# Attention and two MoE layers on one core: the score matmuls of the third and fourth batch written for two tiles of queries at a time

## The chip, the core and the metric

The kernel runs on one core of one Trainium2 chip. Its time is the device time of one execution in microseconds (us), the median of several runs. A core has a matrix engine (TensorE, PE in the profile, with its weight loads shown apart as PEld), a vector engine (VectorE, DVE), a scalar engine (ScalarE, ACT), a general engine (GpSimd, POOL) and a queue engine (SyncE, SP) that here issues nearly all DMAs. Each engine executes its own instructions in the order in which they stand in its program, and waits where an operand or a buffer isn't ready; what stands behind a waiting instruction on the same engine waits with it. Matmuls write to banks of PSUM, and a bank can be written anew only when its last reader is through.

## The reference

Attention over 4 batches of 12 heads (448 queries, head size 64), with queries and keys normalised, and behind it two MoE layers over all 1792 tokens. Cut to what is computed:

```python
q_n, k_n = rmsnorm(q, g_q), rmsnorm(k, g_k)
scores = q_n @ k_n.T / sqrt(64)
attn = exp(scores - max(scores));  attn = attn / (attn.sum() + 1e-9)
x = (attn @ v)                       # -> 1792 x 768
g = x @ w_gate;  val = x @ w_val     # 768 -> 1536
x = (silu(g) * val) @ w_out          # 1536 -> 768
h = x @ w_in                         # 768 -> 2048
out = (h * cos(h)) @ w_out2          # 2048 -> 768
```

## The kernel before, in words

All values are float32 outside; inside, a float32 operand is split into two float16 parts, and a product is three float16 matmuls. Two heads are taken at a time (a pair): one in partitions and columns 0 to 63, the other in 64 to 127. A batch has 6 pairs, and a pair has 7 tiles of queries (64 queries of both heads), so that a batch has 42 tiles.

The scores of one tile are four matmuls with 64 columns of weights each and 448 columns moving, into one PSUM bank: two (one per head) with weights from `T`, the transposed and split queries and keys, and two with weights from `W`, a copy of `T` with its halves swapped. `s_mm` writes them. Behind them, for the tile, `s_max` takes the largest score of a row on DVE, `s_exp` (line 518) reads the bank once more on ACT and writes `pr`, and that frees the bank; then `pr` is split into float16 parts (`p`, line 542 and a subtraction on DVE or POOL), transposed by a DMA (`PT`), and multiplied with the values (`t<-PT,vh` and `t<-PT,vl`, again with 64 columns of weights). The banks of the scores are a pool of three, `ps_s`, which the small matmuls for the scales of the weights (`nm`) share; a tile's matmuls wait until the bank of three allocations before is free.

The first and second batch's scores stand at the start of the program and are written by another function. Those of the third and of the fourth batch are computed while the matrix engine works at the first MoE layer of the batches before them: the loop over `visits` writes, at each visit of a piece of weights (gate, value, output), some calls of `step`, which for a running number `n` calls `s_mm(n)`, `s_max`, `s_exp` and the later parts for tiles some steps back, and then the MoE matmuls (`mm<-xy,wp`, 128 columns of weights) into two banks of the pool `ps_m`, which has four. When a piece is through, `fin_gate` (lines 1153 and 1154) or `fin_val` (line 1162) reads these two banks on ACT and DVE, and its last reading on DVE (`ga`) frees them. DVE also converts the weights of later pieces to split form (`w<-raw`, `w<-raw,w`, then `wp<-w`).

The order of instructions on an engine isn't the order in which they are written: a scheduler sets it when the program is built, after its own estimate of when operands come ready. `tc.keep_in_program_order(r)` pins an instruction behind the one that was written just before it on the same engine. The helper `InOrder` does so for all instructions of an engine while the engine's name is in the set `in_order`; for PE this holds until the fourth visit, so that in the third and fourth batch the scheduler sets PE's order.

All operations that go through the helper have the line number 166 in the profile.

Of the kernel before, what the change touches and what calls it, by code (L numbers as in the profile page):

```python
# [174 lines left out]
def kernel(ctx: ExitStack, tc, q, k, v, g_q, g_k, w_gate, w_val, w_out, w2_in, w2_out, out):  # L175
    nc = tc.nc
    in_order = set()
    sync = InOrder(tc, nc.sync, "SP", in_order)
    gps = InOrder(tc, nc.gpsimd, "POOL", in_order)
    pe = InOrder(tc, nc.tensor, "PE", in_order)  # L180
    vec = InOrder(tc, nc.vector, "DVE", in_order)
    dve = InOrder(tc, nc.vector, "DVE0", in_order)
    B, H, S, D = q.shape
# [11 lines left out]
    HP = P // 2  # L195
# [22 lines left out]
    ps_s = ctx.enter_context(tc.tile_pool(name="ps_s", bufs=3, space=PSUM))  # L218
# [13 lines left out]
    def bank(pool, tag):  # L232
        return pool.tile([P, 512], F32, tag=tag, name=tag)
# [70 lines left out]
    NS = 2 * S // P  # L304
# [9 lines left out]
    slot = {}  # L314
# [172 lines left out]
            )  # L487

    def s_mm(n):
        g, t = divmod(n, NS)  # L490
        pg = prep[g]
        if t == 0:
            sms[g] = pools["sm"].tile([P, 3, 8], F32, tag="sm", name="sm")
        ps = bank(ps_s, "s")
        T, W = pg["T"], pg["W"]
        for i in range(2):
            for h in ((0, 1), (1, 0))[i]:
                hs = slice(HP * h, HP * h + HP)
                pe.matmul(
                    ps[hs, :S].rearrange("p (t q) -> p t q", q=HP), (T, W)[i][:, t, hs], T[:, NS:, hs],  # L500
                    start=(i == 0), stop=(i == 1),
                )
        slot[n] = ps

    def s_max(n):
        g, t = divmod(n, NS)
# [356 lines left out]
    def step(n, b):  # L863
        if b == 0:
            c_step(n)
        elif NB * b <= n < NB * (b + 1):
            s_mm(n)
            s_max(n)
            s_tail(n, b, 0)
            s_exp(n)  # L870
            s_tail(n, b, 1)
            s_prep(n)
        elif n >= 0:
            s_tail(n, b, 0)
            s_tail(n, b, 1)
        else:
            s_prep(n)
# [587 lines left out]
    for n in range(NBEGIN * NS - LEAD, NCB + CXX + CXL + 1):  # L1465
# [6 lines left out]
        i = n - EARLY  # L1472
# [44 lines left out]
    for bn, per in blocks:  # L1517
# [15 lines left out]
        for qn in range(per):  # L1533
            i = i0 + qn
# [53 lines left out]
    for c in range(NH):  # L1588
        j0 = j
        j += 2  # L1590
        for b in range(B):
            ps = [bank(ps_s, "s"), bank(ps_t, "t")] if nh % 3 == 2 else [bank(ps_m, "mm") for _ in range(2)]
# [41 lines left out]
    ps = {}  # L1634
# [55 lines left out]
```

## Time and profile before

| what | value |
|---|---|
| time, median of 3 runs | 1250.65 us (1249.37 to 1251.18) |
| profiled execution | 1257.0 us, of it 1255.2 us the span on the core |
| mean granted TensorE clock | 0.984 of full |
| busy | PE 1171.8 us (93%), DVE 944.2 us (75%), ACT 711.4 us (57%), POOL 377.2 us (30%) |
| scores of the third batch on PE | about 217 to 476 us of the span |
| scores of the fourth batch on PE | about 530 to 660 us of the span |

A row of the timeline reads: start in us, duration from the first start to the last end, engine, line, operation, output from inputs, partitions x columns of the weights, size and type of the output, and x with the number of instructions alike in a row; in brackets stands the idle time of the engine just before and who ended it. On PE the durations overlap, since one matmul flows in while another flows out; the rate is read from the starts.

### The profile page before, as it was taken

Reading aid. Unit: us, or ns where it says so; the run is one execution under the profiler, and the core shown is the slowest. Engines: PE = TensorE matmul, PEld = TensorE weight load, DVE = VectorE, ACT = ScalarE, POOL = GpSimd, SP = SyncE. Lnnn points to the kernel's source line nnn. Section 1 sums busy time; section 2 is a strip of 40 time slices with the busy share of each in tenths; the row PEclk is TensorE's granted clock in tenths of the full one; section 3 lists DMA queues with packets and bytes.
Section 4 is the critical chain, followed back from the end, with each engine's and each line's share of the span. In section 5 each row is a group of like instructions: output and inputs, shape, how many; then the busy total and the mean of one; then the engine's idle time right before and its main releaser. Section 6 shows DMA issues by size and latency. Waiting matters only on the chain. (4 is left out here: it accounts for less than half of the span.)

```text
span 1255.2 us, 18124 instructions
## 1 busy us (share of the span) xinstructions
PE 1171.8 (93%) x6294; PEld 658.5 (52%) x6294; DVE 944.2 (75%) x1778; ACT 711.4 (57%) x1356; POOL 377.2 (30%) x309
## 2 busy tenths in 40 slices
PE   2888988999998999999999999999999999999998
PEld 1333333445763447844468544865555554666655
DVE  7888865697668897068864498657888788999882
ACT  4878875545665653356653355457677667666220
POOL 7734503535322265035553012612112221100000
PEclk9989999999999999999999999999999999999999
DMA  7476665368767879589767687770522235222122
GB/s 189 113 187 191 174 190 162 81 187 251 191 197 216 216 194 308 180 180 232 158 139 238 231 307 284 263 245 9 209 69 76 89 139 201 63 95 76 51 70 88
DMA packets 220304, 211.47 MB, mean 168 GB/s; under 512 B 147124, under 2 KB 177716, under 8 KB 220212
## 3 DMA queue, kind: packets, MB, share of 16 engines
q1 hardware_dynamic: 220208, 210.31, 58.0%
q8 instruction: 49, 0.80, 0.3%
q14 instruction: 43, 0.35, 0.1%
q10 hardware_dynamic: 4, 0.00, 0.0%
HBM read 138.38 MB, written 41.57 MB: 143 GB/s over the span
## 5 line engine op out<-in xcount | busy, mean ns | idle before, releaser
L166 PE MATMUL mm<-xy,wp 128*128 128x448 f16 x2484 | 492.7, 355 | 8.2 <-DVE ga L1154 5.3
L166 PEld LDWEIGHTS <-wp 128*128 128x128 f16 x2880 | 278.0, 99 | 282.3 <-issue 38.6
L166 PE MATMUL mm<-g,wp 128*128 128x448 f32 x864 | 185.0, 371 | 1.9 <-DVE ga L1162 1.9
L166 PEld LDWEIGHTS mm<-g,wp 128*128 128x128 f32 x864 | 161.8, 190 | 21.2 <-issue 4.2
L166 DVE SCALAR_TENSOR_TENSOR w<-raw,w 128x768 int32<-128x768 int32 x136 | 144.9, 1071 | 1.2
L166 DVE TENSOR_REDUCE sm<-s 128x1 f32<-128x448 f32 x168 | 100.4, 614 | 50.6 <-PE s L166 50.4
L166 PEld LDWEIGHTS <-g 128*128 128x128 f16 x840 | 82.1, 98 | 55.4 <-DVE tmp L166 0.7
L166 POOL TENSOR_TENSOR g<-ga,g 128x448 fp32r<-128x448 f32 x48 | 67.0, 1406 | 144.4 <-ACT g L1164 144.1
L166 POOL TENSOR_TENSOR g<-tmp,g 128x224 f16<-128x224 f32 x64 | 48.0, 753 | 199.2 <-ACT g L1281 198.9
L518 ACT ACTIVATE pr<-s,sm,esc 128x448 f32<-128x448 f32 x84 | 60.4, 720 | 78.2 <-DVE sm L166 70.3
L166 PE MATMUL s<-T 128*64 128x448 f16 x336 | 63.6, 394 | 27.7 <-DVE T L166 16.9
L166 POOL TENSOR_TENSOR wp<-w,wp 128x768 fp32r<-128x768 f32 x36 | 70.7, 1971 | 58.5 <-ACT wp L1042 39.7
L166 DVE TENSOR_SCALAR w<-raw 128x768 int32<-128x768 int32 x68 | 49.4, 731 | 48.4 <-POOL wp L166 14.1
L166 PEld LDWEIGHTS <-T 128*64 128x64 f16 (+1 forms) x432 | 28.2, 109 | 104.6 <-issue 82.9
L166 POOL TENSOR_TENSOR ri<-ss,half 128x14 f32<-128x14 f32 x24 | 64.1, 2673 | 52.7 <-DVE ss L166 51.3
L973 ACT ACTIVATE raw<-w 128x768 f32<-128x768 f32 x56 | 47.0, 838 | 43.5 <-DVE w L166 30.7
L1274 ACT ACTIVATE tmp<-tmp 128x448 f32<-128x448 f32 x64 | 36.3, 571 | 50.3 <-DVE tmp L1273 49.2
L166 POOL TENSOR_TENSOR p<-pr,p 128x448 f16<-128x448 f32 x36 | 39.9, 1114 | 82.0 <-ACT p L542 63.3
L166 PE MATMUL mm<-wp,g 128*128 128x384 f16 x360 | 62.1, 326 | 0.6 <-DVE tmp L166 0.4
L166 POOL TENSOR_TENSOR h<-rqk,h 128x448 f16<-128x448 f32 x32 | 37.4, 1176 | 82.1 <-ACT h L447 52.8
L166 PE MATMUL s<-wp,g 128*128 128x384 f16 x360 | 61.9, 326 | 0.0
L166 PE MATMUL t<-pr,cV 128*128 128x448 f32 (+1 forms) x96 | 51.8, 623 | 9.1 <-ACT pr L722 8.5
(197 smaller groups left out, 1930.5 us busy)
## 6 DMA issues: line engine op xcount, KB each, us to landing
raw<-in_moe_w_out_dram SPq DMA_DIRECT2D x28, 768.0 KB, 5.7
raw<-in_moe_w_in_dram SPq DMA_DIRECT2D x16, 768.0 KB, 6.8
raw<-in_moe_w_gate_dram SPq DMA_DIRECT2D x12, 768.0 KB, 6.7
raw<-in_moe_w_val_dram SPq DMA_DIRECT2D x12, 768.0 KB, 5.3
wp<-scr_gate SPq DMA_DIRECT2D x24, 384.0 KB, 4.1
w<-scr_out SPq DMA_DIRECT2D x24, 384.0 KB, 3.8
wp<-scr_val SPq DMA_DIRECT2D x24, 384.0 KB, 5.3
y<-tmp SPq DMA_DIRECT2D x30, 224.0 KB, 3.8
```

What stands on the lines that cost most here:

```text
L166: r = f(*args, **kw)
L518: nc.scalar.activation(e, slot.pop(n)[:, :S], AF.Exp, bias=sm[:, 1, t:t + 1], scale=esc, accum_out=sm[:, 2, t:t + 1],)
L973: nc.scalar.activation(sq_dst[0], w32, AF.Square, accum_out=n[:, 0:1])
L1274: nc.scalar.activation(r, r, AF.Abs)
```

## The change

`s_mm(n)` at an even tile of a pair (0, 2, 4, 6) takes the banks of that tile and of the next, and writes the matmuls of both, eight in a row, each but the first pinned behind the one before it. At an odd tile it returns at once. Tile 6 has no partner and is written alone. So the pair's 28 matmuls are written as runs of 8, 8, 8 and 4 in place of seven runs of 4. The scheduler may still put other matmuls between two of a run. The instructions themselves are the same in kind and number on every engine.

```diff
     def s_mm(n):
+
         g, t = divmod(n, NS)
         pg = prep[g]
         if t == 0:
             sms[g] = pools["sm"].tile([P, 3, 8], F32, tag="sm", name="sm")
-        ps = bank(ps_s, "s")
+        if t % 2:
+            return
         T, W = pg["T"], pg["W"]
-        for i in range(2):
-            for h in ((0, 1), (1, 0))[i]:
-                hs = slice(HP * h, HP * h + HP)
-                pe.matmul(
-                    ps[hs, :S].rearrange("p (t q) -> p t q", q=HP), (T, W)[i][:, t, hs], T[:, NS:, hs],
-                    start=(i == 0), stop=(i == 1),
-                )
-        slot[n] = ps
+        run = []
+        for m in range(t, min(t + 2, NS)):
+            ps = slot[n + m - t] = bank(ps_s, "s")
+            for i in range(2):
+                for h in ((0, 1), (1, 0))[i]:
+                    hs = slice(HP * h, HP * h + HP)
+                    r = pe.matmul(
+                        ps[hs, :S].rearrange("p (t q) -> p t q", q=HP), (T, W)[i][:, m, hs], T[:, NS:, hs],
+                        start=(i == 0), stop=(i == 1),
+                    )
+                    if run and "PE" not in in_order:
+                        tc.keep_in_program_order(r)
+                    run.append(r)
```

On PE, the first two tiles of the third pair of the third batch (at 293.79 and 297.80 us in the trace before). `s_3054` is the bank of tile 0, `T_2850` and `W_2949` the pair's weights, `mm_3014` a bank of the MoE matmuls. Before:

```order
L166 LDWEIGHTS T_2850
L166 MATMUL s_3054<-T_2850 64x448
L166 LDWEIGHTS W_2949
L166 MATMUL s_3054<-T_2850,W_2949 64x448
L166 LDWEIGHTS W_2949
L166 MATMUL s_3054<-T_2850,W_2949 64x448
L166 LDWEIGHTS wp_2741
L166 MATMUL mm_3014<-xy_1312,wp_2741 128x448
```

The same place after, where `s_3059` is the bank of tile 1:

```order
L166 LDWEIGHTS W_2949
L166 MATMUL s_3054<-T_2850,W_2949 64x448
L166 LDWEIGHTS T_2850
L166 MATMUL s_3059<-T_2850 64x448
L166 LDWEIGHTS T_2850
L166 MATMUL s_3059<-T_2850 64x448
L166 LDWEIGHTS W_2949
L166 MATMUL s_3059<-T_2850,W_2949 64x448
L166 LDWEIGHTS W_2949
L166 MATMUL s_3059<-T_2850,W_2949 64x448
L166 LDWEIGHTS wp_2741
L166 MATMUL mm_3014<-xy_1312,wp_2741 128x448
```

Tile 1 stood 18 MoE matmuls later before, in a run of four of its own; now it follows tile 0 directly. Counted over the whole program, stretches of 64-column matmuls (scores, products with the values, or both) between two 128-column matmuls are 82 before (44 of them in the third batch, 38 in the fourth) and 64 after (29 and 35). Some runs of eight are cut by the scheduler: of the fourth batch's first tile one matmul stands some 160 matmuls ahead of the other three.

On DVE, the same pair (at 299.98 to 308 us in the trace before). `sm_3053<-s_3054` and `sm_3053<-s_3099` are the row maxima of tiles 0 and 1, `ga_2974` and `ga_2977` the readings of line 1162 that free two MoE banks, `W_3363<-T_3266` the copies for a later pair. Before:

```order
L166 TENSOR_REDUCE sm_3053<-s_3054 128x1
L166 TENSOR_SCALAR sm_3053<-sm_3053,nesc_96 128x1
L166 TENSOR_TENSOR p16_3106<-pr_3065,p16_3106 128x448
L1162 SCALAR_TENSOR_TENSOR ga_2974<-ga_2974,gs_2972,mm_3014 128x448
L1162 SCALAR_TENSOR_TENSOR ga_2977<-ga_2977,gs_2972,mm_3015 128x448
L166 TENSOR_REDUCE sm_3053<-s_3099 128x1
L166 TENSOR_SCALAR sm_3053<-sm_3053,nesc_96 128x1
L166 COPY W_3363<-T_3266 64x896 x2
L166 TENSOR_TENSOR h16_3545<-rqk_3263,h16_3545 128x7x64
```

The same place after (line 1169 is what line 1162 was):

```order
L166 COPY W_3363<-T_3266 64x896 x2
L166 TENSOR_TENSOR h16_3545<-rqk_3263,h16_3545 128x7x64
L166 TENSOR_REDUCE sm_3053<-s_3054 128x1
L166 TENSOR_REDUCE sm_3053<-s_3059 128x1
L166 TENSOR_SCALAR sm_3053<-sm_3053,nesc_96 128x1 x2
L1169 SCALAR_TENSOR_TENSOR ga_2974<-ga_2974,gs_2972,mm_3014 128x448
L1169 SCALAR_TENSOR_TENSOR ga_2977<-ga_2977,gs_2972,mm_3015 128x448
L166 TENSOR_TENSOR p16_3106<-pr_3070,p16_3106 128x448
```

The two copies and the subtraction for a later pair now stand ahead of the maxima of tiles 0 and 1 and of the two `ga`.

On DVE again, near the end of the third batch (457.91 to 468.30 us in the trace before). `ga_4712`, `ga_4715` and `ga_4789` are readings of line 1154 that free MoE banks, `w32_` the conversions of later weights. Before:

```order
L166 SCALAR_TENSOR_TENSOR wp_4686<-w32_4484,wsc_101,wp_4686 128x768
L166 TENSOR_SCALAR w32_4682<-raw_4583 128x768
L1154 SCALAR_TENSOR_TENSOR ga_4712<-ga_4712,mm_4602 128x448
L166 TENSOR_SCALAR w32_4795<-raw_4647 128x768
L166 SCALAR_TENSOR_TENSOR w32_4682<-raw_4583,w32_4682 128x768
L1154 SCALAR_TENSOR_TENSOR ga_4715<-ga_4715,mm_4603 128x448
L166 TENSOR_REDUCE sm_4365<-s_4718 128x1
L166 SCALAR_TENSOR_TENSOR w32_4795<-raw_4647,w32_4795 128x768
L166 TENSOR_SCALAR w32_4832<-raw_4753 128x768
L166 SCALAR_TENSOR_TENSOR w32_4682<-raw_4583,w32_4682 128x768
L166 TENSOR_SCALAR sm_4365<-sm_4365,nesc_96 128x1
L166 SCALAR_TENSOR_TENSOR w32_4795<-raw_4647,w32_4795 128x768
```

After, where `ga_4717` and `ga_4720` are the same two readings of the banks `mm_4602` and `mm_4603`:

```order
L1161 SCALAR_TENSOR_TENSOR ga_4717<-ga_4717,mm_4602 128x448
L166 TENSOR_SCALAR nm_4638<-s_4635 128x1
L166 TENSOR_SCALAR nm_4638<-nm_4638 128x1
L166 TENSOR_SCALAR winv_100<-nm_4638 128x1
L166 RECIPROCAL wsc_101<-winv_100 128x1
L1166 TENSOR_SCALAR gs_4715<-winv_100,vsc_102,gs_4715 128x1
L1161 SCALAR_TENSOR_TENSOR ga_4720<-ga_4720,mm_4603 128x448
L1166 TENSOR_SCALAR gs_4787<-winv_100,vsc_102,gs_4787 128x1
L166 TENSOR_TENSOR p16_4725<-pr_4729,p16_4725 128x448
L166 SCALAR_TENSOR_TENSOR wp_4643<-w32_4427,wsc_101,wp_4643 128x768
L166 SCALAR_TENSOR_TENSOR wp_4691<-w32_4484,wsc_101,wp_4691 128x768
L166 TENSOR_SCALAR w32_4687<-raw_4588 128x768
```

Both readings stand ahead of the weights' scaling and of the conversions now, where before they stood among these.

## Rows read from the trace of the kernel before

**Rows 1.** The page: busy us, share of the span and instructions of each engine.

```profile
PE 1171.8 (93%) x6294; PEld 658.5 (52%) x6294; DVE 944.2 (75%) x1778; ACT 711.4 (57%) x1356; POOL 377.2 (30%) x309
```

**Rows 2.** Busy time by stretch: window, length, busy of each engine, PEclk, DMA share, GB/s.

```profile
254.00:300.00 46.00, 44.25 (x244) 21.04 (x244) 43.63 (x76) 22.85 (x45) 21.81 (x13) 0.96 0.76 214
347.00:400.00 53.00, 48.05 (x251) 28.95 (x248) 36.90 (x82) 32.05 (x70) 11.45 (x9) 0.94 0.73 203
400.00:476.00 76.00, 71.08 (x409) 34.86 (x410) 70.56 (x125) 38.89 (x77) 33.27 (x22) 1.00 0.83 220
530.00:600.00 70.00, 69.12 (x410) 31.11 (x407) 51.28 (x108) 40.94 (x89) 28.16 (x22) 1.00 0.88 204
```

**Rows 3.** PE's timeline, a run of four scores and an idle stretch.

```profile
297.52 0.35 PE L166 MATMUL mm<-xy,wp 128*128 128x448 f16 x1
297.80 0.38 PE L166 MATMUL s<-T 128*64 128x448 f16 x2
298.01 0.36 PE L166 MATMUL s<-T,W 128*64 128x448 f16 x2
298.30 0.74 PE L166 MATMUL mm<-xy,wp 128*128 128x448 f16 x3
```

**Rows 4.** PE's timeline, a run of eight scores that stands in before already.

```profile
527.76 2.06 PE L166 MATMUL mm<-xy,wp 128*128 128x448 f16 x10
529.75 0.38 PE L166 MATMUL s<-T 128*64 128x448 f16 x2
...
530.34 0.35 PE L166 MATMUL s<-T,W 128*64 128x448 f16 x2
530.63 3.58 PE L166 MATMUL mm<-xy,wp 128*128 128x448 f16 x18
```

**Rows 5.** What PE waited for, 217 to 490 us: total us, times, longest us.

```profile
PE s L166 <- ACT pr L518: 6.5, 3, 3.2
PE mm L166 <- DVE ga L1154: 5.3, 4, 2.0
PE mm L166 <- DVE ga L1162: 1.9, 2, 1.5
```

**Rows 6.** PE's timeline, waits late in the third batch and just behind it.

```profile
464.71 6.59 PE L166 MATMUL mm<-xy,wp 128*128 128x448 f16 x34 [2.00 <-DVE ga L1154]
472.10 6.02 PE L166 MATMUL mm<-xy,wp 128*128 128x448 f16 x31 [0.80 <-DVE ga L1154]
...
487.00 0.68 PE L166 MATMUL mm<-g,wp 128*128 128x448 f32 x2 [1.54 <-DVE ga L1162]
```

**Rows 7.** DVE's timeline, where line 1162 frees banks near 281 us.

```profile
280.37 0.67 DVE L1162 SCALAR_TENSOR_TENSOR ga<-ga,gs,mm 128x448 f32<-128x448 f32 x1
...
282.95 2.68 DVE L166 SCALAR_TENSOR_TENSOR w<-raw,w 128x768 int32<-128x768 int32 x3
```

**Rows 8.** DVE's timeline at the third pair's first tiles.

```profile
299.98 0.62 DVE L166 TENSOR_REDUCE sm<-s 128x1 f32<-128x448 f32 x1
...
304.14 0.62 DVE L166 TENSOR_REDUCE sm<-s 128x1 f32<-128x448 f32 x1
...
306.77 0.79 DVE L166 COPY W<-T 64x896 f16<-64x896 f16 x2 [1.77 <-DMA T<-h]
307.60 0.62 DVE L166 TENSOR_TENSOR h<-rqk,h 128x448 f16<-128x448 f32 x1
```

**Rows 9.** PE's timeline, the wait at 347 us.

```profile
346.86 0.38 PE L166 MATMUL s<-T 128*64 128x448 f16 x2 [3.21 <-ACT pr L518]
```

**Rows 10.** DVE's timeline, 460 to 467 us.

```profile
460.24 0.61 DVE L1154 SCALAR_TENSOR_TENSOR ga<-ga,mm 128x448 f32<-128x448 f32 x1
460.77 1.65 DVE L166 TENSOR_SCALAR w<-raw 128x768 int32<-128x768 int32 x1
462.34 1.78 DVE L166 SCALAR_TENSOR_TENSOR w<-raw,w 128x768 int32<-128x768 int32 x1
464.05 0.61 DVE L1154 SCALAR_TENSOR_TENSOR ga<-ga,mm 128x448 f32<-128x448 f32 x1
```

## The prediction, as it was written before the change was run

> **What bounds the kernel now.** I read the page's busy shares first: PE is busy 1171.8 of 1255.2 us [rows 1], so what PE does not have to do, or does not have to wait for, is the only thing that can shorten the program by much. Then the table by stretch [rows 2], since the change touches two of them. In the fourth batch (530 to 600 us) PE is busy 69.12 of 70 us with DVE at 51.28: here PE alone is the bound, and a saving on PE should come through. In the third batch it isn't so. From 254 to 300 DVE is busy 43.63 of 46 us and from 400 to 476 it is 70.56 of 76, as close to full as PE, and from 347 to 400 PE idles 5 us. The view of waits says for whom [rows 5]: for banks that ACT's exponential frees (6.5 us in three waits) and for banks that DVE's `ga` frees (5.3 and 1.9). A saving on PE ahead of such a wait makes the wait longer and nothing else, so the third batch is counted apart from the fourth.
>
> **What one merger saves.** PE's timeline gives the price of leaving the 128-column matmuls for a run of scores and coming back. Matmuls in a stream start 0.19 us apart (ten in 2.06 us, the last 0.35 long, [rows 4]). Around a run of four, the last matmul before starts at 297.52 and the first one behind at 298.30 [rows 3]: 0.78, of which 0.19 would pass anyway, so 0.59. Around the run of eight the last matmul before starts at 527.76 + 9 x 0.19 = 529.47, the first behind at 530.63 [rows 4]: 1.16, so 0.97. Two fours made one eight save 2 x 0.59 - 0.97 = 0.21 us. The two ways into and out of the run are what is saved: they take 0.28 and 0.29 in place of 0.19.
>
> The Trainium skill ("TensorEngine Tiling (Array Packing)", Key Properties) says more strongly that changing the tiling mode drains TensorE, and "TensorE: Matmul & The Clock Gate", Single matmul latency, gives the constant part of a lone matmul as some 166 ns; an estimate by that is 2 x 0.166 = 0.33 us a merger and 6.0 us for the eighteen below. Rows 3 and 4 show 0.09 to 0.10 us a change, not 0.166, and the sum goes by them.
>
> **How many mergers.** Written in pairs, 84 runs of four would become 48 runs. The order gives less, since in before some runs stand together or beside products with the values already, and in after the scheduler cuts some: 82 stretches become 64. That is 15 fewer in the third batch and 3 in the fourth: 3.15 and 0.63 us, 3.8 together. Nothing is added or taken on any engine; all else is order.
>
> **What moves on the other engines.** (a) A tile's maximum and exponential come in twos, and the second tile of a run needs its bank one step earlier than before. With three banks the lines that PE waits for there are the exponentials, 6.5 us in before [rows 5]; the pair's first tile is computed no later than before, its second earlier, so I count no more than (b) and (c) for it.
>
> (b) Near 281 us the two `ga` of line 1162 stood at 280.37 and a little later, ahead of three conversions of weights that take 2.68 us [rows 7]; now conversions stand ahead. The banks they free are wanted by the next piece but one. Bounds 0 (PE comes late) and 2.7; DVE is 95% busy there, so it can't catch up, and I take 1.5, a little over the middle.
>
> (c) At the third pair's first tiles the copies `W<-T` and the subtraction `h` now stand ahead of two maxima and two `ga`. In before the copy waited 1.77 us for its DMA and ran at 306.77, the subtraction at 307.60 [rows 8], which ends near 308.2. Two maxima (0.62 each, [rows 8]) and their scaling behind it put the first `ga` near 309.6, where it was near 303.0, between the maxima at 299.98 and 304.14: 6.6 us late if the DMA lands as before. That DMA stands earlier on SP's queue too, behind a store and ahead of several transposes; if it comes up to 4 us sooner the delay is 2.7. Queued behind the waiting copy are all of DVE's later work, the exponentials of both tiles on ACT, and the third tile's run on PE, which wants the first tile's bank. Bounds 0 and 6.6; I take 2.7.
>
> (d) Between 460 and 472 us the opposite happens. PE waited 2.00 and 0.80 us for `ga` of line 1154 [rows 6], which on DVE stood among conversions of 1.65 and 1.78 us [rows 10]; now the first two `ga` stand ahead of these. The 2.8 us go. Next is the wait of 1.54 us at 487.00, for `ga` of line 1162 [rows 6]: DVE has the same work to do before it, but for one conversion (about 0.9 us) that is put behind it. So of the 2.8 us 0.9 are kept; bounds 0 and 2.8.
>
> **The sum.** Up to 347 us PE loses 1.5 + 2.7 = 4.2 and saves about half of the third batch's 3.15, so it is 2.6 late. At 346.86 it waited 3.21 us for an exponential [rows 9], and a PE that comes 2.6 later just waits less: the lateness is gone, and with it the saving. The other half, 1.6, falls into 347 to 476, where ACT's and DVE's waits (the rest of the 6.5 and the 5.3, [rows 5]) set the pace: I keep none of it as its own, but the 0.9 of (d). In the fourth batch the 0.63 comes through. Sum: -0.9 - 0.6 = -1.5 us. The profiled execution took 1257.0 us, with a span of 1255.2, some 6 above the median of 1250.65; the sum is a difference and is taken over to the median as it is: 1249.1.
>
> **The rivals.**
>
> A, the saving is kept in full: PE is the bound in the third batch too. For it: PE is 91 to 96% busy there as well [rows 2], and DVE's maxima wait for PE's scores, so that an earlier PE makes an earlier DVE. Then 3.8 to 3.8 + 2.8 (d) are gained: 1246.8 to 1244.0. Against it: 95% and 93% of DVE [rows 2].
>
> B, slower: the copy of (c) holds DVE. Price 6.6, and 2.7 of (b) with it, 9.3, less the 3.8 saved: up to 5.5 us, 1256.2. It decides from the point where PE is later at 347 us than the 3.21 it waited there [rows 9], that is, when the transposed `T` lands about as late as in before, or when the exponential that PE waits for there is itself pushed back with DVE, so that the wait absorbs nothing; the second alone gives 2.6 late less the 1.6 saved behind and the 0.6 of the fourth batch, about +0.5, and both together 4 to 5.5. I put it at 1252.5 to 1256.2. The Trainium skill speaks on this side ("TensorEngine Tiling (Array Packing)", PSUM Bottleneck): tiling makes TensorE faster but not the emptying of PSUM. Rows 5 agree: the banks' readers are PE's main waits there.
>
> C, it does less than it says: the scheduler cuts the runs (one of the fourth batch's first run stands 160 matmuls ahead of its fellows), DVE takes all that the third batch saves, (b) to (d) cancel. Then 1250.2 to 1251.
>
> **How the numbers follow.** The forecast, part of the saving absorbed, 0.40; A 0.25; B 0.26; C 0.09. No change is what lies within 0.2%, 2.5 us, about what a measurement of this kernel can tell. The forecast's own range is 1246.8 to 1251.6; 0.15 of its 0.40 lies below 1248.15, and 0.25 within. A is all faster, B all but 0.01 slower, C the same. Faster 0.15 + 0.25 = 0.40, same 0.25 + 0.01 + 0.09 = 0.35, slower 0.25. The range leaves out the far ends of A and of B, about one in ten each: 1244.5 to 1255.5.
>
> **What would show it.** The runs of scores: a run of eight must take about 1.16 us from the last matmul ahead to the first behind, and the fourth batch must be 0.6 us shorter from 530 us on; if it takes longer, the price is wrong. (b): a wait of PE for `ga` near 285 to 290 us. (c): DVE's copy `W<-T` near 303 to 307 us with idle time ahead of it and PE waiting for `pr` behind; if the copy runs without a wait, B falls. (d): the waits of 2.00 and 0.80 us gone and that near 487 us longer. If PE's waits in the third batch sum to no more than in before, A is right. The prediction is wrong if the third batch ends over 3 us earlier or later, measured from the products with the first gate weights to the first scores of the fourth batch; or if stretches behind 660 us, where nothing is written otherwise, move by more than 1 us.

## The result, and the profile after

The changed kernel takes 1257.81 us (median of 4 runs, 1257.34 to 1260.88) against 1250.72 before: a ratio of 1.0064, with an interval of 1.0046 to 1.0081. It is slower, by 7 to 8 us, and lies outside the range given. On another chip it measured 1.0044 (1.0024 to 1.0064, the run `after2` below).

The profiled execution took 1257.94 us, span 1256.2. It can't be set against the first profile of before by its span (1255.2), because up to 217 us, where the two programs are the same, that execution is 4.65 us behind the changed kernel's, at a lower clock (0.94 against 0.97). A second profile of before (`again`, below) has a span of 1251.2 us and serves as the base from here on.

The table by stretch of the changed kernel, as [rows 2] of before (window, length, busy time of each engine, PEclk, DMA share, GB/s):

```profile
254.00:300.00 46.00, 42.17 (x224) 20.01 (x225) 42.38 (x69) 21.98 (x44) 19.92 (x12) 0.93 0.85 232
347.00:400.00 53.00, 50.73 (x285) 31.27 (x285) 39.17 (x88) 32.94 (x74) 13.65 (x9) 0.94 0.83 219
400.00:476.00 76.00, 71.10 (x390) 34.89 (x389) 67.42 (x123) 39.32 (x79) 27.71 (x20) 0.98 0.80 200
530.00:600.00 70.00, 67.70 (x397) 30.75 (x395) 47.26 (x97) 37.01 (x83) 27.06 (x20) 1.00 0.83 198
```

From 254 to 300 us PE got through 224 matmuls where before it was 244, and DVE did less too: both wait more. PE's waits from 217 to 490 us, as [rows 5] (total us, times, longest):

```profile
PE mm L166 <- DVE ga L1169: 7.1, 6, 2.5
PE s L166 <- ACT pr L525: 6.8, 3, 3.9
PE t L166 <- DMA PT<-p: 3.1, 2, 2.5
...
PE mm L166 <- DVE ga L1161: 0.3, 1, 0.3
```

Line 1154 of before is line 1161 now, 1162 is 1169, and 518 is 525. The waits for line 1154 are gone (5.3 us before, 0.3 now), those for line 1162 grew from 1.9 to 7.1.

Where the time went is best seen from PE's matmuls themselves, since nearly all of the MoE matmuls stand in the same order in both programs. For a place in the span of `again`, the table gives how much later (in us) the MoE matmuls nearest to it start in another profile, with the lateness at 217 us taken as 0.

```
place      before  after  after2  third  third_a  third_b  after_pinall
254          0.3   -0.5    -1.0   -0.9     -2.0     -0.5      -2.0
272          0.3    5.3     4.7    4.8      1.6     -0.6      -4.1
341         -0.4    6.1     4.3    5.1      2.9     -0.6      -1.5
347          1.0    9.2     8.2    8.6      5.4      2.0       2.6
385          0.0    7.1     6.1    6.5      4.4     -0.1       0.5
400         -0.2    0.1    -1.1   -1.3     -3.5     -5.2      -7.3
425         -0.2   -0.1    -1.3   -1.4     -2.4     -3.7      -6.4
440          0.3    4.4     3.1    3.9     -5.7     -0.3      -3.1
476         -0.3    2.1     0.8    3.0     -2.0     -3.1      -3.3
500         -0.3    7.1     5.9    5.0     -1.8     -4.3      -2.3
530         -0.3    6.0     4.8    3.8     -1.8     -4.3      -3.3
660         -0.4    7.4     7.1    8.4     -1.1     -3.3      -3.7
1240         1.8    7.3     6.8    8.6      3.3      0.4      -4.0
```

Each column is one execution. The first, before against before, differs by 1 us up to 660 us and by 2 behind it; but behind 660 us, where nothing is written otherwise, `third_a` falls back by 4.4 us and `third_b` by 3.7, so there the table can't be trusted to less than 4. The profiled executions of the changed kernel, `after2`, `third`, `third_a` and `third_b` are within 1.2 us of the median of their runs. That of `after_pinall` isn't: at 1249.01 us it is the fastest of ten, with a median of 1253.99. In the changed kernel four steps make the loss (254 to 272, 272 to 347, 425 to 440, 476 to 500), and one takes 7 us of it back (385 to 400).

**The saving is there.** A run of eight in the changed kernel, on PE's timeline:

```profile
247.67 0.92 PE L166 MATMUL mm<-xy,wp 128*128 128x448 f16 x4
248.52 0.38 PE L166 MATMUL s<-T 128*64 128x448 f16 x2
...
249.12 0.36 PE L166 MATMUL s<-T,W 128*64 128x448 f16 x2
249.40 0.93 PE L166 MATMUL mm<-xy,wp 128*128 128x448 f16 x4
```

The last of the four matmuls ahead starts at 247.67 + 3 x 0.19 = 248.24, the first behind at 249.40: 1.16 us, as in [rows 4]. The new runs of eight are all in the third batch: from 217 to 505 us PE executes 41 runs of four and none of eight in before, and 15 of eight and one of ten in the changed kernel. From 505 to 670 us the scheduler had joined fours already, 11 runs of eight in before against 9 now.

**The waits that ate it.** PE's timeline of the changed kernel at the four steps, with the idle time ahead in brackets:

```profile
265.74 2.83 PE L166 MATMUL t<-PT,vh 128*64 128x448 f16 x14 [2.53 <-DMA PT<-p]
...
319.38 12.80 PE L166 MATMUL mm<-g,wp 128*128 128x448 f32 x54 [1.93 <-DVE ga L1169]
...
431.97 0.61 PE L166 MATMUL s<-nm,full 128*128 128x1 f32 x4 [3.95 <-ACT pr L525]
...
486.79 2.64 PE L166 MATMUL mm<-g,wp 128*128 128x448 f32 x7 [2.51 <-DVE ga L1169]
```

and PEclk (the third number from the end) in the 5 us at each of them:

```profile
265.00:270.00 5.00, 4.26 (x25) 1.97 (x26) 5.00 (x8) 1.51 (x3) 2.64 (x2) 0.66 0.50 167
320.00:325.00 5.00, 5.00 (x19) 4.48 (x18) 2.85 (x2) 0.65 (x2) 5.00 (x3) 0.66 1.00 226
430.00:435.00 5.00, 3.03 (x12) 1.60 (x13) 3.71 (x11) 4.75 (x12) 1.03 (x1) 0.76 0.78 263
485.00:490.00 5.00, 3.21 (x11) 2.17 (x13) 4.70 (x9) 1.73 (x3) 2.58 (x2) 0.72 0.85 263
```

Each of these waits is paid twice in this execution. Behind it the granted clock falls to its lower level, 1.2 GHz, for part of the slice: the 14 products with the values that take 1.51 us elsewhere take 2.83 at 265.74, which is 1.3 us on top of the wait of 2.53. The Trainium skill ("TensorE: Matmul & The Clock Gate", HAM oscillation) tells of the same in a kernel that waits for DMAs again and again: the work behind each wait starts at the lower clock, so that the wait is paid once more each time. The trace agrees at these four places (waits of 1.93 to 3.95 us), but not at each wait. In `after2` the clock doesn't fall at the second (1.12 us at 319.2), and in `third_a` the products of the first come after a longer wait and take 1.51:

```profile
264.95 1.51 PE L166 MATMUL t<-PT,vh 128*64 128x448 f16 x14 [3.46 <-DMA PT<-p]
```

**The first step is a queue that the prediction did not look at.** SP's queue in the changed kernel and then in `again`, where the transpose is the one that the products at 265.74 and at 261.37 need last:

```profile
254.87 0.92 SPq L166 DMA_DIRECT2D raw<-in_moe_w_out_dram  x2
255.84 0.48 SPq L166 DMA_DIRECT2D scr_out<-w  x1
256.41 1.66 SPq L166 DMA_TRANSPOSE PT<-p  x1
```

```profile
257.11 1.23 SPq L166 DMA_TRANSPOSE PT<-p  x1
...
259.69 0.38 SPq L166 DMA_DIRECT2D raw<-in_moe_w_out_dram  x1
...
261.58 0.54 SPq L166 DMA_DIRECT2D raw<-in_moe_w_out_dram  x1
```

In the new order the transpose stands directly behind two loads of 768 KB and a store of 384. The view of its transfers gives its landing, 9.3 us after it was issued. In `again` the landing of its counterpart isn't recorded; its products run 4.3 us after it was issued without waiting, and the recorded landings of the transposes from 235 to 275 us are 3.9 to 5.3 us (changed kernel first, then `again`):

```profile
DMA to landing us min/median/max: 9.3/9.3/9.3
```

```profile
DMA to landing us min/median/max: 3.9/4.0/5.3
```

Six of the profiles have this order on SP (`after`, `after2`, `third`, `third_a`, `after_pin18`, `after_pinh`), and each has a wait of 2.5 to 3.7 us at this place, with 9.0 to 9.3 us to landing. Of the others only `fix8` has both loads and the store ahead of the transpose, with one more small transfer between (6.5 us to landing, a wait of 2.88); no other waits over 0.4 us for this transpose. Two loads alone don't make the wait: in `after_gsw` the transpose behind them lands after 6.3 us, in time. The Trainium skill ("DMA: Bandwidth & Descriptors", Queues, rings and completion order) says that a DMA engine consumes the descriptors of a ring in ring order; the 9.3 us agree with it.

**The third step is rival B, at another pair than the one named.** DVE and then ACT of the changed kernel ahead of the wait at 431.97:

```profile
428.83 0.79 DVE L166 COPY W<-T 64x896 f16<-64x896 f16 x2 [3.16 <-DMA T<-h]
429.65 0.62 DVE L1161 SCALAR_TENSOR_TENSOR ga<-ga,mm 128x448 f32<-128x448 f32 x1
430.19 1.15 DVE L166 TENSOR_REDUCE sm<-s 128x1 f32<-128x448 f32 x2
```

```profile
428.83 0.58 ACT L433 ACTIVATE h<-rqk 128x448 f16<-128x448 f32 x1 [3.19 <-DMA T<-h]
...
431.12 0.71 ACT L525 ACTIVATE pr<-s,sm,esc 128x448 f32<-128x448 f32 x1
431.73 0.19 ACT L525 ACTIVATION_READ_ACCUMULATOR pr<-s,sm,esc 128x1 f32 x1
```

The copies wait for the transposed `T`, two maxima wait behind them on DVE, and on ACT the exponential waits behind a write of `h` that can't start before the same transpose has read the old `h`. The bank comes free at 431.9, and PE has waited 3.95 us.

### The profile page after: what moved, and what is told of

The parts are those of the page before. It is cut to its first block, busy times and chain, and to the rows that moved or that the text cites. A ratio compares the mean times of both kernels' runs of the same rounds, so it can differ in the third digit from the quotient of the medians.

```text
span 1256.2 us, 18128 instructions
## 1 busy us (share of the span) xinstructions
PE 1168.1 (93%) x6294; PEld 660.5 (53%) x6294; DVE 943.1 (75%) x1778; ACT 709.0 (56%) x1356; POOL 376.7 (30%) x309
## 5 line engine op out<-in xcount | busy, mean ns | idle before, releaser
L166 POOL TENSOR_TENSOR g<-ga,g 128x448 fp32r<-128x448 f32 x48 | 63.3, 1333 | 102.7 <-ACT g L1171 102.6
L166 DVE TENSOR_SCALAR w<-raw 128x768 int32<-128x768 int32 x68 | 49.5, 733 | 41.6 <-POOL wp L166 20.2
L1161 DVE SCALAR_TENSOR_TENSOR ga<-ga,mm 128x448 f32<-128x448 f32 x46 | 27.4, 611 | 43.8 <-ACT ga L1160 43.7
```

The costliest lines, as they stand in the source:

```text
L166: r = f(*args, **kw)
L1161: nc.vector.scalar_tensor_tensor(t, t, 1.0, ps[f][:, :S], op0=ALU.add, op1=ALU.mult)
```

## The experiments

Each result is the ratio to before on the same chip, with its 95% interval in brackets. Two theories stood against each other at first. "Order": a run of eight saves what it was priced at, and the loss comes from the waits that the scheduler's new order makes. "Banks": a run of two tiles needs two of the three banks, wherever it stands. Built without the two lines that pin the run's matmuls, the program has the same order on all five engines, and so has before with its runs of four pinned; the pins do nothing here, and the change is the pairs alone.

**Before again.** The kernel unchanged.

> The kernel before, unchanged, for a second profile. In the first one TensorE's granted clock was 0.94 over the first 217 us, where the profile of the changed kernel has 0.97, though the program is the same there; the changed kernel is 4.65 us ahead at 217 us. Both theories expect this profile to be nearer 1250 us than 1257, with the start some 4 to 5 us shorter and the same waits as before behind 217 us: 1.98 at 254.5, 3.21 at 346.9, 2.58 and 1.60 at 390, 2.00 at 464.7, each at its place in the program.

1252.94 us, span 1251.2. The waits of before came back at their places (2.07 at 252.3, 3.21 at 345.1, 2.83 and 1.20 at 388 to 391, 2.17 at 462.7). At the first, second and last of these the clock didn't fall this time, and at 252.3 and 345 it had in the first profile.

**One batch alone.** For the third batch (the fourth: `g // NP > 2`):

```diff
-        if t % 2:
+        two = 2 if g // NP < 3 else 1
+        if t % two:
             return
...
-        for m in range(t, min(t + 2, NS)):
+        for m in range(t, min(t + two, NS)):
```

> Runs of two tiles in the third batch alone; the fourth batch's scores are written as before, four matmuls per step. [...] Theory 'banks' (a run of two tiles takes two of the three banks of the scores at once, wherever it stands): the loss goes by the number of runs, half of it here, 3 to 4 us slower.

1.0063 (1.0039 to 1.0088): the whole loss. Not all of it arises in the third batch: by the table 3.8 of 8.4 us stand at 530 us, and 4.6 come up to 660, in the fourth batch, whose scores are written as before but ordered anew. There PE waits 7.9 us, against 2.9 in `again`.

> Runs of two tiles in the fourth batch alone; the third batch's scores are written as before. By the order of the program the number of runs of scores in the fourth batch stays 31, since the scheduler had joined pairs there in before. Theory 'order': no more than 1.5 us slower than before, and less at the end, 1250 to 1252. Theory 'banks': the other half of the loss, 3 to 4 us slower, 1254.

1.0013 (0.9995 to 1.0031): the fourth batch alone costs 1.6 us, which can't be told from nothing. Half of the loss each, as "banks" had it, isn't what was measured. As a test of "banks" the run is weak, though: PE executes the runs of before in it, 11 of eight and 20 of four in the fourth batch.

**Paired the other way.**

```diff
-        if t % 2:
+        if t and t % 2 == 0:
             return
...
-        for m in range(t, min(t + 2, NS)):
+        for m in range(t, min(t + 1 + (t > 0), NS)):
```

> Runs of two tiles in both batches, but paired the other way: tile 0 alone, then 1 and 2, 3 and 4, 5 and 6. As many runs of eight are written as in the changed kernel. Theory 'banks': the same loss as the changed kernel, 1256 to 1259, with PE waiting for exponentials. Theory 'order': the waits stand at other places and sum to something else; the time is off 1257.8 by 3 us or more, either way.

1.0052 (1.0035 to 1.0069), as slow as the changed kernel, which "order" hadn't expected, but with the waits at other places: none at 265, 4.44 us for a bank at 391, 2.50 at 435, 2.83 for a maximum at 478. These are read in its fastest execution of ten (1255.14 us, the median is 1260.49), so the trace leaves 5 us unshown. Inconclusive by itself.

**Half of the third batch each** (`12 <= g < 15` and `15 <= g < 18` in the line above).

> Runs of two tiles in the first three pairs of the third batch alone; all else is written as before. Theory 'order' (the loss sits at a few places where the redrawn order makes PE wait, and in the clock that falls behind the wait): PE is 8 to 9 us late at 347 us, from a wait for PT at 265, one for ga near 319 and their clock, as in the changed kernel; before's own waits for banks and for weights at 388 to 391 us (4 us and a lower clock) then take back 4 to 7 of it: 1 to 4 us slower than before at the end. Theory 'banks' (each run of two tiles costs, by holding two of the three banks): half of the third batch's loss, 4 us slower, spread over all six places where runs of eight stand.

1.0013 (0.9996 to 1.0030).

> Runs of two tiles in the last three pairs of the third batch alone. Theory 'order': nothing moves before 347 us; from there the changed kernel gained 7 us to 400 us and lost 6 to 530 us. Since the gain to 400 us was the lateness absorbed, this kernel doesn't get it: 3 to 6 us slower, from the wait for a bank at 432 us (4 us and its clock) and those for ga at 475 to 487 us. Theory 'banks': the other half, 4 us slower, with PE waiting for exponentials wherever runs of eight stand.

1.0001 (0.9985 to 1.0017), better than either theory expected (3 to 6 us and 4 us slower). The halves together cost 2 us and the whole 8. The table suggests how: before has waits of its own at 388 to 391 us (4 us and a lower clock). The first half is 4.4 us late at 385 and loses that lateness there; the second half comes in time and gains 5 us there, which pays for the wait at its end of the batch. With both halves the gain is spent on the lateness of the first, and the loss at 425 to 440 is left to pay. That is an account of one execution each, and it goes to 660 us, where the halves are 1.1 and 3.3 us ahead of `again`; they lose that lead behind it, where the changed kernel loses nothing, and why stays open. "Banks" falls here: runs of eight in number cost nothing by themselves.

**Banks, tried directly.** The small matmuls for the scales of the weights leave the scores' banks, in before and in the changed kernel:

```diff
-        ps = bank(ps_s, "s")
+        ps = bank(ps_t, "t") if y_pool == [] and g_pool else bank(ps_s, "s")
         for i, n in enumerate(q):
```

> The kernel before, with one thing moved: the small matmuls for the scales of the weights take the bank of the products with the values in place of one of the scores' three banks, while the third and fourth batch are computed. It is the base for the next run. Before waited at 388 us (2.6 to 2.8 us, for a bank that an exponential frees). Theory 'banks': that wait and its lower clock go, 2 to 4 us faster than before. Theory 'order': the wait goes but others come, within 3 us of before, either way.

1.0051 (1.0033 to 1.0070).

> The changed kernel (runs of two tiles in both batches) with the same move: the scores have their three banks to themselves. Theory 'banks': the wait of 4 us at 432 us goes with its clock and PE's waits for exponentials fall from 8.9 us to under 4; the time falls from about 1258 to 1252 or less, no slower than the kernel before with the same move. Theory 'order': the single wait goes, but this kernel stays 3 us or more behind the kernel before with the same move.

1.0060 (1.0040 to 1.0079). A bank more for the scores helps neither, and the kernel before gets 6 us slower by it, with no run of eight added, which neither theory allowed: PE waits 2.38 us at 261 and 1.84 at 362 for the bank that the two uses now share. The two are as far from before as the changed kernel is, and from each other by nothing that can be measured.

**PE's order pinned.** Through both batches, with runs of four and with runs of eight:

```diff
         else:
+            in_order.clear()
             attn_ctx.close()
...
             if i == 3:
-                in_order.clear()
+                in_order.intersection_update(("PE",))
```

> PE's order is taken from the scheduler: through the whole third and fourth batch every instruction of PE is pinned behind the one written before it; the scores are written four matmuls per step, as in the kernel before. The other engines are ordered by the scheduler as ever. It is the base for the next run, with 71 stretches of 64-column matmuls. Both theories leave its own time open, since before's order is another: 1250 to 1270 us.

1286.87 us.

> The same pinned order of PE with the changed kernel's runs of two tiles, all of them whole: 48 stretches of 64-column matmuls in place of 71, so 23 fewer, 4.8 us at 0.21 each. Theory 'order' (a run of eight saves what it was priced at; what costs is which waits the scheduler's new order happens to make, and the clock that falls behind the longer ones): 1 to 5 us faster than the run with fours in the same pinned order. Theory 'runs' (a run of eight itself makes PE wait, since the second tile comes a step sooner than its bank and its readers can follow): 3 us or more slower than the run with fours.

1275.85 us, 11 us less than with fours (1.0165 against 1.0249, intervals 1.0132 to 1.0199 and 1.0208 to 1.0290). So long as PE's order is the same but for the runs, eights are not slower (the other engines' order is still the scheduler's, and differs). But the gain isn't the 4.8 us of the mergers: by the same kind of table the eights are level or 1 us behind at 530 us, and gain it all in the fourth batch, where with fours PE waits 14.0 us for three transposes and with eights 1.0. In the third batch 18 stretches fewer brought nothing: PE waits 23.4 us there with fours and 32.2 with eights. What PE saves there it waits.

**One run of eight alone**, at the start of the third batch and in its fifth pair:

```diff
-        if t % 2:
+        if (g, t - 1) in TWO:      # TWO = {(12, 0)}, then {(16, 1)}
             return
+        two = 2 if (g, t) in TWO else 1
...
-        for m in range(t, min(t + 2, NS)):
+        for m in range(t, t + two):
```

> One run of eight alone, tiles 0 and 1 of the first pair of the third batch; all other scores as before. It saves one stretch (0.2 us), but 13 matmuls that aren't scores, 46 instructions on DVE, 19 on ACT and 10 DMAs stand elsewhere in the order than before. Theory 'order': time moves by more than the 0.2 us, 1 to 6 us slower, as with the moved bank of the scales. Theory 'runs': a thirtieth of the loss, so within 1 us of before.

1.0003 (0.9985 to 1.0020).

> One run of eight alone at another place, tiles 1 and 2 of the fifth pair of the third batch; 15 matmuls that aren't scores and 33 instructions on DVE stand elsewhere. Theory 'order': 0 to 4 us slower than before. Theory 'runs': within 1 us of before.

1.0006 (0.9987 to 1.0025). Small changes of the order cost nothing; "order" in the form that any new draw costs some us falls.

**The copies `W<-T` away from DVE.** In the third batch, in both kernels:

```diff
+            eng = gps if g // NP == 2 else dve
-            dve.tensor_copy(W[:HP], T[HP:, :NS])
-            dve.tensor_copy(W[HP:], T[:HP, :NS])
+            eng.tensor_copy(W[:HP], T[HP:, :NS])
+            eng.tensor_copy(W[HP:], T[:HP, :NS])
```

> The changed kernel with the third batch's copies W<-T on GpSimd in place of DVE, so that no maximum and no ga stands behind a DVE instruction that waits for the transposed T. In the profiles of the changed kernel and of the runs of two tiles in the third batch alone, DVE waits 8.6 us at these copies and ACT 23 us at the writes of h for the same transposes, against 7.7 and 10 in before, and at 428 us of the latter the wait for a bank (4.85 us, PE's longest) is the end of that chain. Theory 'copies' (the loss of the changed kernel is mainly rival B of the prediction, the maxima behind a copy that waits): 4 us or more faster than the changed kernel, 1250 to 1254. Theory 'spread' (many waits share the loss and each new order draws others): within 3 us of the changed kernel or of the next run plus 4 to 8 us.

1.0025 (1.0008 to 1.0041).

> The kernel before with the same move of the copies W<-T to GpSimd, as the base for the run above. Theory 'copies': 0 to 3 us faster than before, since before waits 7.7 us there but few of PE's waits hang on it; the two kernels with copies on GpSimd within 2 us of each other. Theory 'spread': within 6 us of before, either way, and 4 us or more faster than the changed kernel with the same move.

1.0034 (1.0014 to 1.0054). The two are level, where without the move they are 7 us apart; but before lost 4 us by it, and in the changed kernel PE still waits 8.7 us for exponentials, 4.0 at the longest. The wait at 265 is gone: the transposes are issued at 252.81 us, and the products run at 259.29 without a wait.

**The copies pinned.** On one chip with the changed kernel again:

> The changed kernel, unchanged, for a second profile and for its time on the same chip as the three runs below. Both theories: 0.4 to 0.8% slower than before; a wait of 3 to 5 us for a bank of the scores at the place of 432 us, behind DVE's copies and ACT's write of h that wait for the transposed T.

1259.07 us, 1.0044 (1.0024 to 1.0064). Its waits are those of the first profile: 3.66 at 266.8, 1.12 at 319.2, 3.86 at 432.2, 2.50 at 487.1.

```diff
-            dve.tensor_copy(W[:HP], T[HP:, :NS])
-            dve.tensor_copy(W[HP:], T[:HP, :NS])
+            for d, h in ((W[:HP], T[HP:, :NS]), (W[HP:], T[:HP, :NS])):
+                r = dve.tensor_copy(d, h)
+                if g == 18:
+                    tc.keep_in_program_order(r)
```

> The changed kernel with the two copies W<-T of the fourth batch's first pair pinned behind the DVE instruction written before them: on DVE they leave the place at 428.8 us, where they waited 3.2 us ahead of a ga and two maxima, and stand 38 instructions later; 6 instructions on DVE, 2 on ACT and 1 matmul move with them, nothing else. ACT's write of h, which waits for the same transpose 3.2 us, with the exponentials behind it, stays. Theory 'copies on DVE alone': PE's wait at 432 us goes, 3 to 6 us faster than the changed kernel. Theory 'both engines wait for the transpose': ACT still holds the exponentials, PE's wait stays at 3 us or more, within 1.5 us of the changed kernel.

1.0059 (1.0040 to 1.0078), and PE's wait for the bank is 4.15 us as before. This edit moves the least (6 instructions on DVE, 2 on ACT, 1 matmul), and its answer is plain: the copies on DVE alone do not hold PE at 432 us; ACT's write of `h`, which waits for the same transpose, was left in its place, and the wait stayed.

With ACT's write of the next pair's `h` pinned as well:

```diff
-            nc.scalar.activation(h16[:, NS:, 0:D], k3, AF.Copy)
+            r = nc.scalar.activation(h16[:, NS:, 0:D], k3, AF.Copy)
+            if g == 19:
+                tc.keep_in_program_order(r)
```

> As the run above, with ACT's write of the next pair's h pinned too, so that neither the copies nor the write of h stand ahead of the maxima and exponentials at 432 us. The pin moves more of the order (71 matmuls, 70 on DVE, 32 on ACT). Theory 'both engines wait for the transpose': PE's wait at that place falls to under 1 us; 3 to 6 us faster than the changed kernel unless the rest of the order brings new waits. Theory 'spread': within 3 us of the changed kernel.

1.0039 (1.0020 to 1.0059). PE's wait there is 3.18 us, not under 1; the step at 476 to 500 is gone (0.5 us gained there in place of 5 lost), but PE comes 4.3 us later from 530 to 660 us, and 4.3 more by 1240. No gain over `after2` that can be measured.

With all six pairs' copies pinned (`13 <= g <= 18`, without the pin on `h`):

> The changed kernel with the copies W<-T of six pairs (the last five of the third batch and the first of the fourth) pinned behind the DVE instruction written before them, so that none stands ahead of maxima of earlier steps; 48 matmuls, 104 instructions on DVE, 31 on ACT move. Theory 'copies': DVE's wait at copies falls from 8.6 us to under 4, 3 to 6 us faster than the changed kernel, as with the copies on GpSimd. Theory 'spread': within 3 us of the changed kernel.

1253.99 us, 1.0004 (0.9984 to 1.0024): the loss is gone, 5.1 us against `after2`, and the runs of eight are as many as in the changed kernel or more (60 stretches of 64-column matmuls against 64; 16 runs of eight from 217 to 505 us against 15). SP's queue and PE's timeline at the first and the third step:

```profile
252.90 1.22 SPq L166 DMA_TRANSPOSE PT<-p  x1
254.22 0.56 SPq L166 DMA_DIRECT2D raw<-in_moe_w_out_dram  x1
255.37 0.42 SPq L166 DMA_DIRECT2D raw<-in_moe_w_out_dram  x1
```

```profile
257.58 0.57 PE L166 MATMUL t<-PT,vh 128*64 128x448 f16 x4
...
424.72 0.61 PE L166 MATMUL s<-nm,full 128*128 128x1 f32 x4 [1.42 <-ACT pr L527]
```

The transpose stands ahead of the loads again, the products follow 4.7 us behind its issue with no wait, and the wait for the bank is 1.42 us. But DVE's waits at copies add up to 6.6 us, not to under 4, and the pins moved 104 instructions on DVE, 31 on ACT and 48 matmuls. So this run shows that the same runs of eight can cost nothing in another order; it doesn't show that the copies' own waiting was the price.

## Why the prediction was wrong, point by point

The forecast was 1.5 us gained; 7 to 8 were lost. The sign that it had set for itself shows it: the third batch ends 6.0 us late at 530 us (4.8 in `after2`), over the 3 allowed.

- **The price of a merger** (0.21 us) and **their number** (15 and 3) were right.
- **The sum as a sum over places named by hand** was the step that failed. It took three places ((b), (c), (d)) for all that the new order changes, and in (a) counted nothing more for the banks that the exponentials free, one of which then cost 3.95 us at 432. So it had PE 2.6 us late at 347 us, where the table has 9.2, and 0.9 us gained from there to 530 us, where 4.5 us are lost at 425 to 440 and 5.0 at 476 to 500. The largest single step, 254 to 272 us (5.8 us), had no term at all: I looked at SP's queue only for `T`, not for the transposes `PT` and the loads ahead of them. The new order of that queue, set against the rows on SP, could have shown it.
- **(b)**, priced 1.5: PE waits 0.16 us near 282. Too dear.
- **(c)**, priced 2.7 with bounds of 0 and 6.6: at the third pair the copies ran at 299.33, not at 306.77 [rows 8], since the transpose came that much sooner, and PE waited 0.62 us for it. The bounds held there, the place was wrong: the same queueing took 3.95 us and a lower clock at 432, at the copies for the fourth batch's first pair. Rival B (0.26) had named it at the one place (c), though each pair has such copies; B had the direction right, but it ends at 1256.2 us, and its mechanism shows at two places, here and at 347 (below), of all that was lost.
- **(d)**: the waits of 2.00 and 0.80 us [rows 6] are gone, and PE gained 2 us from 440 to 476, nearly the 2.8 worked out. The next wait was put at 1.9 us more than before's 1.54, for a net gain of 0.9. It came as three (0.44, 0.76, 2.51 us, the last two for what was line 1162) with a lower clock, and the step from 476 to 500 us costs 5.0.
- **The absorption** was right in kind and wrong in place. At the wait of 3.21 us at 347 [rows 9], where the sum had all lateness gone, none went: PE is 6.1 us late ahead of it (341) and 7.1 behind it (385). The exponential was pushed back too, as rival B's second condition has it: a copy that waits for `T` stands ahead of a maximum on DVE, PE still waits 2.20 us, then 1.22 more, and the clock falls (PEclk 0.73 and 0.59 from 345 to 350 and 350 to 355). DVE, then PE:

```profile
343.48 0.79 DVE L166 COPY W<-T 64x896 f16<-64x896 f16 x2 [2.45 <-DMA T<-h]
344.31 0.62 DVE L166 TENSOR_REDUCE sm<-s 128x1 f32<-128x448 f32 x1
```

```profile
347.45 0.59 PE L166 MATMUL s<-T 128*64 128x448 f16 x2 [2.20 <-ACT pr L525]
...
350.59 2.83 PE L166 MATMUL t<-PT,vh 128*64 128x448 f16 x14 [1.22 <-issue]
```

  The waits at 388 to 391 took 7.0. But they served only once, as the halves show: lateness that arises behind them stays.
- **The clock** had no term. Before has waits too, but from 217 to 535 us in both profiles of the changed kernel the clock falls at 265, at 347 to 355, at 432 and at 487 us, and in the first also at 255 and 320; in before it falls at three places in the first profile (256, 348, 392) and at one in `again` (387 to 394). PEclk from 217 to 535 us, in before, `again`, the changed kernel and `after2`:

```profile
217.00:535.00 318.00, 299.71 (x1628) 180.91 (x1625) 230.58 (x415) 165.07 (x350) 119.66 (x78) 0.98 0.72 200
217.00:535.00 318.00, 297.71 (x1627) 179.65 (x1625) 230.18 (x414) 164.53 (x350) 119.22 (x78) 0.99 0.73 201
217.00:535.00 318.00, 297.16 (x1596) 182.57 (x1595) 228.81 (x406) 159.01 (x343) 117.00 (x76) 0.96 0.74 199
217.00:535.00 318.00, 295.50 (x1602) 181.08 (x1601) 230.17 (x408) 160.46 (x345) 117.67 (x77) 0.97 0.75 200
```

  Over all runs the mean granted clock is 0.982 (10 runs of `after2`) and 0.984 (4 of the changed kernel) against 0.987 (31 of before on the same chip). Counted from 217 to 535 us, PE's waits add up to 20.7 and 22.4 us in the two profiles of the changed kernel and to 18.2 and 20.2 in those of before. That is 2 us more waiting. What the float16 and float32 matmuls in these stretches take beyond 0.2 us each, where they start over 0.3 us behind the one before without a wait, is 12.0 and 8.7 us against 6.5 and 4.1. With 3.15 us saved by 15 mergers the three give 2.4 + 5.0 - 3.15 = 4.2 us on the mean, where the table shows 5 to 6 at 530 us. By this count the loss is more in the clock than in the waiting.
- **The fourth batch**, forecast at 0.6 us gained: 1.4 lost from 530 to 660 us in this profile and 2.3 in `after2`; alone it is not to be told from no change.

What stays open: why this order of the scheduler, and the one of `odd`, are both 6 to 8 us worse than before's, where those with half of the runs and the one with pinned copies are not. Each has its own waits, and no single one was removed without moving others. Keeping PE busy through a wait, so that the clock stays, wasn't tried, since any instruction more draws the order anew.

## What to carry to other kernels

Where a scheduler orders the program, a change in one place is a change of every queue: go through the order of each queue, DMA queues included, for transfers that now stand behind large loads, before any sum over the places one had in mind. A saving on an engine that waits for others nearby is worth nothing there, and one wait can absorb a lateness only once. Price each wait of PE that is made longer with the clock behind it.

## What the runs showed of the hardware

- Entering and leaving the 64-column runs costs 0.09 to 0.10 us each over the stream's 0.19, no more.
- The same wait is followed by a lower clock in one execution and not in another: 3.21 us at 346.9 in the first profile of before with 0.80 and 0.86 in the slices around it, and 1.00 at the same place in `again`, where these rows are the wait (it ends at 345.1) and what follows:

```profile
343.00:348.00 5.00, 2.90 (x27) 1.85 (x27) 2.38 (x8) 4.01 (x10) 1.03 (x1) 1.00 0.83 213
348.00:353.00 5.00, 5.00 (x27) 4.64 (x27) 0.10 (x1) 0.71 (x2) 1.04 (x1) 1.00 0.55 177
```

- A DMA transpose issued right behind two loads of 768 KB and a store lands after 9.0 to 9.3 us in six profiles; in the changed kernel the other transposes around it landed after about 4.
